# Attention: exponentials ahead of the copies of the transposes, sums of logits behind the next maximum

## The chip, the cores and the metric

The kernel runs on one core of a Trainium2 chip. The core has engines with instruction queues of their own: TensorE (PE in the rows, its weight loads PEld) multiplies matrices, ScalarE (ACT), VectorE (DVE) and GpSimd (POOL) work element by element, and SyncE (SP) issues DMAs here. Each engine takes its instructions in the order of the program and waits on semaphores for those of other engines. Matrix products land in tiles in PSUM; the other tiles of the kernel lie in SBUF. The metric is the device time of one execution in microseconds, the median of three runs.

## What is computed

Three stages follow one another; the change is in the first.

```python
# attention over keys and values averaged in groups of 8: B, H, S, D = 8, 8, 576, 64
k_p = k.reshape(B, H, S // 8, 8, D).mean(axis=3)      # 72 pooled keys a head
v_p = v.reshape(B, H, S // 8, 8, D).mean(axis=3)
scores = np.matmul(q, k_p.transpose(0, 1, 3, 2)) / np.sqrt(D)
attn = np.exp(scores - np.max(scores, axis=-1, keepdims=True))
attn = attn / (np.sum(attn, axis=-1, keepdims=True) + 1e-09)
x = np.matmul(attn, v_p).transpose(0, 2, 1, 3).reshape(B * S, H * D)   # 4608 x 512
# mixture of experts: a skip score decides whether a token is computed, a gate (8 logits) by
# which expert; out = x + gate_w * (relu(x @ w1[e]) @ w2[e])
# rational feed-forward: h = x @ w_in; g = P(h) / Q(h); out = g @ w_out
```

## The kernel before

**Tiles of tokens.** The 4608 tokens are cut into 36 tiles of 128. For each pair of batches there are nine: two blocks of 256 tokens of the first batch (each gives two tiles, the even and the odd tokens), one mixed tile (64 tokens of either batch), and two blocks of the second. A mixed tile needs the keys of two batches, so its score matmuls and its products with v come in twice the number.

**One step of the loop.** The loop runs over `i` from -2 to 35, and its program order is the order on every engine; nothing reorders it. A step works on five tiles at once, in this order:

- `st_B(i + 1)`: TensorE makes the scores of a tile (L392) in the PSUM tile `sc`; VectorE takes the maxima of the eight heads in one reduction (L402). In eight of the steps, one for each batch, TensorE also multiplies the pooled v by the gate's weights (L359) into the same PSUM tile, behind the scores, and VectorE multiplies the result by a mask (L365) behind the maximum. So the product with v gives, beside the 64 columns of a head, its share of the 8 expert logits, of the skip score and of the sum of the exponentials.
- `st_A(i + 2)`: TensorE transposes q (L376) in the PSUM tile with the tag `qT`, ScalarE copies it to SBUF (L378).
- `st_C(i - 1)`: TensorE transposes the exponentials (L421, and L422 for the last 64 of 576) in the PSUM tiles `eT` and `ms`; ScalarE copies both (L424, L425).
- `st_exp(i + 1)`: ScalarE makes the exponentials, eight instructions of 128x72 (L414), one for each head with its own maximum as bias.
- `mark`: VectorE makes two one-hot tables for a tile whose rank is known (L529, L531).
- `st_D(i - 2)`: TensorE multiplies the transposed exponentials by v (L439) in the PSUM tile `pv`.
- `advance`: the router's next stage for a finished group of 8 or 4 tiles. In its third stage TensorE counts tokens by expert (L510) in columns of `ms`; in its fourth VectorE reads them (`val`, L518).
- `finish(i - 2)`, which `st_D` returns: VectorE adds and inverts the sums (L454, L456), scales the logits (L457) and the 512 columns (L460), sums the logits over the heads into `lg` (L466) and into the token's row `xr` (L467), and SyncE stores the rows of a finished pair to `xg` in DRAM (L471, L473). There are two `xr` buffers, one for a pair.
- Behind it: TensorE places the marked tokens (L535), and in certain steps prepares a later batch: it transposes its pooled keys in the PSUM tile `eT` (L332) and the last 64 rows of them in `ms` (L338), and its pooled v in `qT` (L346). ScalarE copies the results (L313, L318, L349).

**What exists once.** The PSUM tiles of this stage are `sc` and `pv` with 2 x 512 numbers in each partition, and `qT`, `eT`, `ms` and the placing table `ix` with 512. Each of them has one buffer. The transposes of keys share theirs with those of the exponentials, the transposes of v with those of q, and the columns of `ms` are shared by three users:

```python
ps = ps1.tile([128, 512], F32, tag="eT", name="kTp")      # prep_k: pooled keys
ps = ps1.tile([128, 4, 128], F32, tag="eT", name="eTp")   # st_C: exponentials
ps = ps1.tile([128, 512], F32, tag="qT", name="vTp")      # prep_v: pooled v
ps = ps1.tile([128, 512], F32, tag="qT", name="qTp")      # st_A: q
ET4, RK0, CN0, KT4 = 0, 264, 345, 354                     # columns of ms
```

Of the kernel before, what the change touches and what calls it, by code (L numbers as in the profile page):

```python
# [26 lines left out]
NT = NTOK // 128  # L27
# [76 lines left out]
def tile_attention_moe_rational_ffn(  # L104
# [92 lines left out]
    with ExitStack() as c1, tc.manual_schedule():  # L197
# [123 lines left out]
        def warm(n):  # L321

            for _ in range(n):
                nc.tensor.transpose(MS[:, 0:128], ident, ident)

        def prep_k(bb):
            kb, kt = kT[bb]
            ps = ps1.tile([128, 512], F32, tag="eT", name="kTp")
            for c in range(4):
                if bb == 0:  # L330
                    warm(6)
                nc.tensor.transpose(ps[:, 128 * c:128 * c + 128], kb[:, c].rearrange("p m d -> p (m d)"), ident)  # L332
            head_block(kt, ps, 0, 512)
# [73 lines left out]
        def st_exp(t):  # L407

            kind, bb, s0, par = TILES[t]
            scv, mx = sc.pop(t)  # L410
            for a in range(2):
                for m in range(4):
                    r, h = (0, 4 * a + m) if kind == "mixed" else (m % 2, 4 * par + 2 * a + m // 2)
                    nc.scalar.activation(out=ex[t][:, r, SP * h:SP * h + SP], in_=scv[:, a, m], func=AF.Exp,  # L414
                                         bias=mx[:, a, m:m + 1], scale=1.0)
# [15 lines left out]
        def st_D(t):  # L431
            ps = ps1.tile([128, 2, 512], F32, tag="sc" if t in (NT - 3, NT - 1) else "pv", name="pvp")
            et = eT.pop(t)
            for p0, n, bb in segs(t):
                for c, h0, nh in PV:
                    np_ = 128 if c < 4 else 64
                    a, hh_ = divmod(h0, 4)
                    m0 = h0 - HEAD0[c]
                    nc.tensor.matmul(ps[p0:p0 + n, a, W * hh_:W * (hh_ + nh)], et[:np_, c, p0:p0 + n],  # L439
                                     vb[bb][:np_, c, m0:m0 + nh, :].rearrange("p m w -> p (m w)"),  # L440
                                     start=h0 in (0, 4), stop=c == 4, skip_group_check=True)
            pv = ps[:, :, 0:4 * W].rearrange("p a (h w) -> p a h w", w=W)
            kind, bb, s0, par = TILES[t]
            if par == 0:
                xr[t] = wk.tile([128, 2, ROW], F32, tag="xr", name="xr")
                if kind == "block":
                    xr[t + 1] = xr[t]
            x_ = xr.pop(t)
            r = wk.tile([128, 2, 4], F32, tag="rs", name="rs")
            l_ = wk.tile([128, H, E + 1], F32, tag="lp", name="lp")  # L450
            rb = r.unsqueeze(3)

            def finish():
                V.tensor_scalar(out=r, in0=pv[:, :, :, W - 1], scalar1=1e-9, scalar2=float(POOL),  # L454
                                op0=ALU.add, op1=ALU.mult)
                V.reciprocal(out=r, in_=r)  # L456
                V.tensor_tensor(out=l_.rearrange("p (a h) e -> p a h e", a=2), in0=pv[:, :, :, D:D + E + 1],  # L457
                                in1=rb.to_broadcast([128, 2, 4, E + 1]), op=ALU.mult)
                if t < NT - 2:
                    V.tensor_tensor(out=x_[:, par, 0:DM].rearrange("p (a h d) -> p a h d", a=2, h=4),  # L460
                                    in0=pv[:, :, :, 0:D], in1=rb.to_broadcast([128, 2, 4, D]), op=ALU.mult)
                else:
                    for h in range(H):
                        nc.scalar.activation(out=x_[:, par, D * h:D * h + D], in_=pv[:, h // 4, h % 4, 0:D], func=AF.Copy,
                                             scale=r[:, h // 4, h % 4:h % 4 + 1])
                V.tensor_reduce(out=lg[:, t, :], in_=l_.rearrange("p h e -> p e h"), axis=AX.X, op=ALU.add)  # L466
                V.tensor_reduce(out=x_[:, par, DM:ROW], in_=l_[:, :, 0:E].rearrange("p h e -> p e h"), axis=AX.X,  # L467
                                op=ALU.add)
                r0 = S * bb + s0
                if kind == "mixed":  # L470
                    nc.sync.dma_start(xg[r0:r0 + 128, :], x_[:, 0, :])  # L471
                elif par:
                    nc.sync.dma_start(xg[r0:r0 + 256, :].rearrange("(p r) f -> p r f", r=2), x_)  # L473

            return finish
# [88 lines left out]
        groups = [(0, 8), (8, 16), (16, 24), (24, 28), (28, 32), (32, 36)]  # L564
        todo = []
        put = []
        prep_k(0)
        warm(6)
        prep_k4(0)
# [8 lines left out]
        for i in range(-2, NT):  # L578
            if i + 5 < NT and i + 5 > 5 and TILES[i + 5][3] == 0:
                load_q(i + 5)  # L580
            for bb in range(B):
                if bb < 2:
                    continue
                if i == max(need[bb] - 11, -2):
                    load_kv(bb, "k")
                if i == need[bb] - 7:
                    load_kv(bb, "v")
                if i == need[bb] - 8:
                    pool_k(bb, nc.gpsimd, nc.gpsimd)()
                if i == need[bb] - 5:  # L590
                    pool_v(bb, (nc.gpsimd, nc.gpsimd))
            if i == 0:
                zero_kt(2, V)
                for c in range(5):
                    rows, n = slice(D * (c % 2), D * (c % 2) + D), min(3, H - HEAD0[c])
                    V.tensor_copy(wg[rows, c, 0:n], wga[rows, HEAD0[c]:HEAD0[c] + n])
            if i == 2:
                V.tensor_copy(tri, cst[:, C_TRI:C_TRI + 128])
                V.tensor_copy(reg, cst[0:1, C_REG:C_REG + NE])
            if i == 3:  # L600
                V.tensor_scalar(out=iob[:, :, 0], in0=iota[:, 0:128], scalar1=-1.0, scalar2=None, op0=ALU.mult)
            if i == 4:
                V.tensor_scalar(out=colb[:, :, 0], in0=iota, scalar1=128.0, scalar2=float(-64 * NCOL), op0=ALU.mult, op1=ALU.add)
            if i == 6:
                nc.sync.dma_start(ab[:, 0:4], a.unsqueeze(0).to_broadcast([128, 4]))
                nc.sync.dma_start(ab[:, 4:6], b.unsqueeze(0).to_broadcast([128, 2]))
            if i == 10:
                nc.gpsimd.tensor_scalar(out=na, in0=ab[:, 0:4], scalar1=-1.0, scalar2=None, op0=ALU.mult)
                nc.scalar.activation(out=bb1, in_=ab[:, 5:6], func=AF.Abs)
            if i == NT - 10:  # L610
                for n in range(NR):
                    load_w(n)
            if i == -1:
                warm(10)
            if 0 <= i + 1 < NT:
                st_B(i + 1, [bb for bb in range(B) if i == need[bb] + (1 if bb else 2)])
            if 0 <= i + 2 < NT:
                st_A(i + 2)
            if 0 <= i - 1 < NT:
                st_C(i - 1)  # L620
            if 0 <= i + 1 < NT:
                st_exp(i + 1)
            if i == 2:
                pool_v(1, (V, V))
            made = [mark(todo.pop(0)) for _ in range(min(len(todo), 1 if i < 28 else 2))]
            ended = st_D(i - 2) if 0 <= i - 2 < NT else None
            for _ in range(1 if i < 32 else 2):
                advance()
            if ended:
                ended()  # L630
            for p_ in put:
                place(*p_)
            if i == 1:
                rest1()
            for bb in range(B):
                if bb and i == need[bb] - (4 if bb > 1 else 2):
                    prep_k(bb)
                if bb and i == need[bb] - (3 if bb > 1 else 2):
                    prep_k4(bb)
                if i == need[bb] - (2 if bb > 1 else 0 if bb else -1):  # L640
                    prep_v(bb)
            put = made
            for g in groups:
                if i - 2 == g[1] - 1:
                    running.append((route(*g), g))
            if NT - 4 <= i < NT:
                split_w(i - NT + 4)
# [4 lines left out]
        for p_ in put:  # L652
            place(*p_)
        ends = [st_D(NT - 2), st_D(NT - 1)]
        ends[0]()
        while len(todo) > 2:
            place(*mark(todo.pop(0)))
        ends[1]()
        for _ in route(*groups[-1]):
            if todo:  # L660
                place(*mark(todo.pop(0)))
# [41 lines left out]
    with ExitStack() as c3, tc.manual_schedule():  # L703
# [271 lines left out]
        ended, begun, uf = small(NU, E), small(NU, E), small(NUT)  # L975
# [107 lines left out]
    with ExitStack() as c4, tc.manual_schedule():  # L1083
# [22 lines left out]
        late = {}  # L1106
# [224 lines left out]
```

## Time and profile before

| | |
|---|---|
| Median of three runs | 1521.79 us (1521.28 to 1528.7) |
| The profiled execution | 1520.28 us, span 1518.5 us |
| Granted TensorE clock, mean over the span | 0.963 |
| TensorE matmuls busy | 1390.6 us (92%) |
| VectorE busy | 1116.5 us (74%) |
| ScalarE busy | 889.2 us (59%) |
| GpSimd busy | 642.4 us (42%) |

The shares are means over all three stages. Scores are made between 13.2 and 199.2 us, so what the change touches is the first eighth of the span; the experts and the feed-forward come behind it and are not touched. A matmul is shown in pipelined form, and the shares are to be read for a stretch, together with what each engine waited for.

### The profile page before, as it was taken

The numbers are of one execution on the slowest core, as the hardware profiler recorded it, in microseconds if no ns is written. First come the engines' busy times: TensorE is split into PE (matmuls) and PEld (weight loads), VectorE is DVE, ScalarE is ACT, GpSimd is POOL, SyncE is SP. The second block draws the span as 40 slices with busy tenths as digits, with TensorE's granted clock in tenths as the row PEclk, the third lists the DMA queues.
The fourth block names the chain that finished last, engine by engine and source line by source line (L and its number), as shares of the span: only waits on it lengthen the run. The fifth ranks groups of instructions, "written<-read, shape, count | busy, mean of one in ns | idle before, by whom it ended". The sixth has DMA issues, their size and how long they took to land.

```text
span 1518.5 us, 21279 instructions
## 1 busy us (share of the span) xinstructions
PE 1390.6 (92%) x6937; PEld 1158.6 (76%) x6937; DVE 1116.5 (74%) x1926; ACT 889.2 (59%) x1805; POOL 642.4 (42%) x575
## 2 busy tenths in 40 slices
PE   7999977879778789997799999999999999999998
PEld 6887856667667677785578888888888888888886
DVE  5478785676667675536998787787878878787885
ACT  4666644344444444335677676776767667676764
POOL 4856226555444443334754233252423325242322
PEclk9999998899979899999999999999999999999999
DMA  9675525556666565341101001010100101010000
GB/s 260 192 223 181 179 76 195 176 184 191 200 209 204 180 209 197 123 129 46 42 1 44 13 28 29 1 56 1 42 14 29 29 1 57 0 43 15 28 1 28
DMA packets 83823, 146.43 MB, mean 96 GB/s; under 512 B 17030, under 2 KB 33866, under 8 KB 83526
## 3 DMA queue, kind: packets, MB, share of 16 engines
q1 hardware_dynamic: 71846, 105.65, 21.7%
q0 software_dynamic: 11680, 37.64, 7.8%
q8 instruction: 86, 1.41, 0.4%
q14 instruction: 211, 1.73, 0.4%
HBM read 117.15 MB, written 27.18 MB: 95 GB/s over the span
## 4 chain that ended last, share of the span: by engine, by line
PE 47%; DVE 5%; ACT 1%; issue 1%; POOL 0%; POOLq 0%; DVEq 0%; ACTq 0%
PE ph L1164 23%; PE py L1222 23%; DVE A L1178 1%; PE px L1147 1%; DVE R L1205 1%; DVE A L1197 1%; DVE R L1201 1%; ACT R L1192 0%; DVE U L1186 0%; ACT R L1193 0%; DVE U L1182 0%; DVE cm L147 0%; POOL out_dram L1228 0%; ACT U L1174 0%; ACT Y L1173 0%
## 5 line engine op out<-in xcount | busy, mean ns | idle before, releaser
L1212 POOL TENSOR_TENSOR GL<-R,GH 128x512 fp32r<-128x512 f32 x143 | 188.0, 1314 | 463.2 <-ACT GH L1211 339.0
L1222 PE MATMUL py<-w0h,GL 128*128 128x512 f32 x576 | 225.2, 391 | 6.6 <-POOL GL L1212 6.6
L1222 PE MATMUL py<-w0h,GH 128*128 128x512 f32 x576 | 226.8, 394 | 0.6 <-issue 0.6
L161 POOL TENSOR_TENSOR w2l<-raw,w2h 128x512 fp32r<-128x512 f32 x90 | 122.3, 1363 | 182.6 <-ACT w2h L160 133.0
L1172 ACT ACTIVATE A<-ph 128x512 f32<-128x512 f32 x140 | 83.0, 593 | 140.7 <-PE ph L1164 140.4
L1178 DVE SCALAR_TENSOR_TENSOR A<-A,bb,Y 128x512 f32<-128x512 f32 x144 | 119.8, 832 | 53.4 <-ACT Y L1173 53.4
L1164 PE MATMUL ph<-xh,w1h 128*128 128x512 f32 x356 | 139.9, 393 | 6.3 <-DVE U L1186 6.3
L1197 DVE SCALAR_TENSOR_TENSOR A<-A,R 128x512 f32<-128x512 f32 x144 | 112.8, 783 | 37.0 <-ACT R L1193 31.0
L1164 PE MATMUL ph<-xl,w1h 128*128 128x512 f32 x356 | 139.4, 392 | 0.0
L1222 PEld LDWEIGHTS py<-w0h,GL 128*128 128x128 f32 x576 | 108.1, 188 | 32.7 <-POOL GL L1212 9.6
L1222 PEld LDWEIGHTS py<-w0h,GH 128*128 128x128 f32 x576 | 108.2, 188 | 22.8 <-issue 0.9
L1211 ACT ACTIVATE GH<-R 128x512 fp32r<-128x512 f32 x144 | 91.9, 638 | 50.8 <-DVE R L1205 50.8
L1205 DVE SCALAR_TENSOR_TENSOR R<-U,ab,R 128x512 f32<-128x512 f32 x144 | 113.1, 785 | 5.1
L1201 DVE SCALAR_TENSOR_TENSOR R<-A,R 128x512 f32<-128x512 f32 x144 | 101.8, 707 | 15.9
L1192 ACT ACTIVATE R<-A,qc 128x512 f32<-128x512 f32 x144 | 104.8, 728 | 14.6 <-DVE A L1178 11.1
L1174 ACT ACTIVATE U<-ph,na 128x512 f32<-128x512 f32 x140 | 109.8, 784 | 0.0
L1186 DVE SCALAR_TENSOR_TENSOR U<-U,ab,ph 128x512 f32<-128x512 f32 x140 | 104.7, 748 | 5.0
L833 PE MATMUL py<-w2h,hh 128*128 128x512 f32 (+2 forms) x240 | 98.9, 412 | 2.4 <-DVE lrow L808 2.4
L845 ACT ACTIVATE hh<-ph 128x256 fp32r<-128x256 f32 (+4 forms) x44 | 19.7, 448 | 136.9 <-PE ph L842 92.1
L833 PE MATMUL py<-w2h,hl 128*128 128x512 f32 (+2 forms) x240 | 96.9, 404 | 2.6 <-DVE hl L846 2.6
L842 PE MATMUL ph<-xh,w1h 128*128 128x256 f32 (+4 forms) x176 | 64.4, 366 | 37.3 <-issue 32.8
L846 DVE SCALAR_TENSOR_TENSOR hl<-ph,hh 128x256 fp32r<-128x256 f32 (+4 forms) x44 | 22.1, 502 | 102.2 <-ACT hh L845 81.6
(328 smaller groups left out, 3812.6 us busy)
## 6 DMA issues: line engine op xcount, KB each, us to landing
raw<-in_moe_w_dram SPq DMA_DIRECT2D x192, 256.0 KB
xg<-xr SPq DMA_DIRECT2D x16, 520.0 KB
q<-in_q_dram SPq DMA_DIRECT2D x16, 512.0 KB
cr<-in_moe_w_in_dram SPq DMA_DIRECT2D x16, 512.0 KB
cr<-in_moe_w_out_dram SPq DMA_DIRECT2D x16, 512.0 KB
k<-in_k_dram SPq DMA_DIRECT2D x7, 1024.0 KB
v<-in_v_dram SPq DMA_DIRECT2D x7, 1024.0 KB
xg<-xr SPq DMA_DIRECT2D x4, 260.0 KB
```

The costliest lines, as they stand in the source:

```text
L161: eng.tensor_tensor(out=dst_lo, in0=src, in1=dst_hi, op=ALU.subtract)
L833: nc.tensor.matmul(PY[j][0:m], l_[:, sl], r_, start=f == 0 and n == 0, stop=f == 7 and n == 2)
L1164: nc.tensor.matmul(ps, l_, r_, start=n == 0, stop=n == 11)
L1174: nc.scalar.activation(out=t["U"], in_=ps, func=AF.Identity, scale=na[:, 3:4], bias=na[:, 2:3])
L1178: nc.vector.scalar_tensor_tensor(out=t["A"], in0=t["A"], scalar=bb1, in1=t["Y"], op0=ALU.mult, op1=ALU.add)
L1186: nc.vector.scalar_tensor_tensor(out=t["U"], in0=t["U"], scalar=ab[:, 1:2], in1=t["h"], op0=ALU.subtract, op1=ALU.mult)
L1192: nc.scalar.activation(out=t["R"], in_=t["A"], func=AF.Ln, bias=qc, scale=1.0)
L1197: nc.vector.scalar_tensor_tensor(out=t["A"], in0=t["A"], scalar=QC, in1=t["R"], op0=ALU.add, op1=ALU.mult)
L1201: nc.vector.scalar_tensor_tensor(out=t["R"], in0=t["A"], scalar=2.0, in1=t["R"], op0=ALU.subtract, op1=ALU.mult)
L1205: nc.vector.scalar_tensor_tensor(out=t["R"], in0=t["U"], scalar=ab[:, 0:1], in1=t["R"], op0=ALU.subtract, op1=ALU.mult)
L1212: (nc.gpsimd if s < tot_ - 1 else nc.vector).tensor_tensor(out=GL, in0=t["R"], in1=GH, op=ALU.subtract)
L1222: nc.tensor.matmul(PY[j], l_[:, sl], r_, start=c == 0 and n == 0, stop=c == NC - 1 and n == 2)
```

## The change

On ScalarE the eight exponentials of a tile (`st_exp`) come ahead of the copy of the transposed q (`st_A`) and of the copies of the transposed exponentials (`st_C`). TensorE's order stays. On VectorE the last part of `finish`, the two sums over the heads, becomes a function `rest`, which runs in the next step behind the next maximum (and behind the mask products L365, where the step has them). The store on SyncE's queue goes with it, and so comes behind the loads of q, k and v that the next step issues. From step 35 on, and for the last two tiles, `rest` runs at once.

```diff
--- before.py
+++ after.py
@@ -463,6 +463,9 @@
                     for h in range(H):
                         nc.scalar.activation(out=x_[:, par, D * h:D * h + D], in_=pv[:, h // 4, h % 4, 0:D], func=AF.Copy,
                                              scale=r[:, h // 4, h % 4:h % 4 + 1])
+                return rest
+
+            def rest():
                 V.tensor_reduce(out=lg[:, t, :], in_=l_.rearrange("p h e -> p e h"), axis=AX.X, op=ALU.add)
                 V.tensor_reduce(out=x_[:, par, DM:ROW], in_=l_[:, :, 0:E].rearrange("p h e -> p e h"), axis=AX.X,
                                 op=ALU.add)
@@ -564,6 +567,7 @@
         groups = [(0, 8), (8, 16), (16, 24), (24, 28), (28, 32), (32, 36)]
         todo = []
         put = []
+        late = []
         prep_k(0)
         warm(6)
         prep_k4(0)
@@ -614,12 +618,14 @@
                 warm(10)
             if 0 <= i + 1 < NT:
                 st_B(i + 1, [bb for bb in range(B) if i == need[bb] + (1 if bb else 2)])
+            if late:
+                late.pop()()
+            if 0 <= i + 1 < NT:
+                st_exp(i + 1)
             if 0 <= i + 2 < NT:
                 st_A(i + 2)
             if 0 <= i - 1 < NT:
                 st_C(i - 1)
-            if 0 <= i + 1 < NT:
-                st_exp(i + 1)
             if i == 2:
                 pool_v(1, (V, V))
             made = [mark(todo.pop(0)) for _ in range(min(len(todo), 1 if i < 28 else 2))]
@@ -627,7 +633,9 @@
             for _ in range(1 if i < 32 else 2):
                 advance()
             if ended:
-                ended()
+                late.append(ended())
+                if i >= NT - 1:
+                    late.pop()()
             for p_ in put:
                 place(*p_)
             if i == 1:
@@ -652,10 +660,10 @@
         for p_ in put:
             place(*p_)
         ends = [st_D(NT - 2), st_D(NT - 1)]
-        ends[0]()
+        ends[0]()()
         while len(todo) > 2:
             place(*mark(todo.pop(0)))
-        ends[1]()
+        ends[1]()()
         for _ in route(*groups[-1]):
             if todo:
                 place(*mark(todo.pop(0)))
```

## Rows read from the trace of the kernel before

**Rows 1.** Busy time by stretches: length, engines' busy time, clock, DMA share, GB/s.

```profile
60.00:80.00 20.00, 18.63 (x134) 16.38 (x133) 11.35 (x39) 14.21 (x56) 14.37 (x15) 1.00 0.55 161
```

**Rows 2.** Maxima and exponentials, 44 to 190 us: who waited for them, us, times.

```profile
  DVE vb L365: 1.7, 1
...
  PE scp L392: 4.9, 10
```

**Rows 3.** Timeline of one ordinary step: start us, length us, engine, line; idle time before.

```profile
60.87 1.25 PE L392 MATMUL scp<-kT,qTs 128*128 128x144 f32 x8
...
61.45 0.27 DVE L466 TENSOR_REDUCE lg<-lp 128x9 f32<-128x72 f32 x1
...
61.64 0.25 DVE L467 TENSOR_REDUCE xr<-lp 128x8 f32<-128x64 f32 x1
...
62.22 0.76 DVE L402 TENSOR_REDUCE mx<-scp 128x8 f32<-128x576 f32 x1 [0.33 <-PE scp L392]
...
62.65 0.60 ACT L378 ACTIVATE qTs<-qTp 128x512 f32<-128x512 f32 x1 [1.35 <-PE qTp L376]
...
62.93 2.02 PE L439 MATMUL pvp<-vb,eTs 128*128 128x148 f32 x12
...
63.14 0.59 ACT L424 ACTIVATE eTs<-eTp 128x512 f32<-128x512 f32 x1
...
63.62 0.26 ACT L425 ACTIVATE eTs<-ms 64x128 f32<-64x128 f32 x1
...
63.78 1.76 ACT L414 ACTIVATE ex<-scp,mx 128x72 f32<-128x72 f32 x8
...
65.58 0.39 PE L392 MATMUL scp<-kT,qTs 128*128 128x144 f32 x1 [0.64 <-ACT ex L414]
```

**Rows 4.** Timeline of TensorE alone, 50 to 88 us.

```profile
52.35 3.67 PE L439 MATMUL pvp<-vb,eTs 128*64 128x148 f32 x24
...
60.16 0.44 PE L346 MATMUL vTp<-ident,vc 128*128 128x128 f32 x2
...
69.60 0.66 PE L332 MATMUL kTp<-ident,kb 128*128 128x128 f32 x4
...
70.31 1.25 PE L392 MATMUL scp<-kT,qTs 128*128 128x144 f32 x8
...
75.78 1.25 PE L392 MATMUL scp<-kT,qTs 128*128 128x144 f32 x8 [0.58 <-ACT ex L414]
...
85.16 0.21 PE L510 MATMUL ms<-oh,tri 128*128 128x72 bf16 x1
...
85.86 1.25 PE L392 MATMUL scp<-kT,qTs 128*128 128x144 f32 x8
```

**Rows 5.** Views of lines L332 and L338: the semaphore waits of TensorE's queue.

```profile
L332 PEldq EVENT_SEMAPHORE  x1: 51/51/51, 68.5 to 68.5; - x1
...
L338 PEldq EVENT_SEMAPHORE  x1: 51/51/51, 74.1 to 74.1; - x1
```

**Rows 6.** Timeline of ScalarE alone, 56 to 92 us.

```profile
67.86 0.59 ACT L424 ACTIVATE eTs<-eTp 128x512 f32<-128x512 f32 x1
...
73.82 0.26 ACT L425 ACTIVATE eTs<-ms 64x128 f32<-64x128 f32 x1
```

**Rows 7.** Timeline of VectorE alone, two stretches.

```profile
72.27 0.76 DVE L402 TENSOR_REDUCE mx<-scp 128x8 f32<-128x576 f32 x1 [0.93 <-PE scp L359]
...
72.95 0.35 DVE L365 TENSOR_TENSOR vb<-scp,cst 128x108 f32<-128x108 f32 x2
...
88.91 0.23 DVE L518 TENSOR_TENSOR val<-ms,oh 128x72 f32<-128x72 f32 x1 [0.93 <-ACT eTs L425]
...
92.47 0.76 DVE L402 TENSOR_REDUCE mx<-scp 128x8 f32<-128x576 f32 x1
```

**Rows 8.** Busy time by stretches, TensorE alone: length, busy time, clock, DMA.

```profile
36.00:38.00 2.00, 0.79 (x5) 1.00 0.08 30
...
38.00:40.00 2.00, 1.63 (x7) 0.61 0.00 0
```

## The prediction

> **What bounds the kernel now.** The change lies in the attention stage, the first 0.2 ms of the span, so I read that stage alone. First the busy time by stretches: between 60 and 80 us TensorE is busy 18.63 of 20 us at its full clock [rows 1]. TensorE nearly sets the pace, and what the change can win is what is left of its waits. Then the view of the maxima and exponentials between 44 and 190 us: TensorE's scores waited for exponentials 10 times, 4.9 us in all [rows 2]. Then one ordinary step in the timeline [rows 3]. Counted from its first score matmul (60.87) the scores end at 1.25, VectorE's maximum runs from 1.35 to 2.11, ScalarE copies the transposed q from 1.78 to 2.38 and the transposed exponentials from 2.27 to 2.86 and 2.75 to 3.01, and runs the exponentials from 2.91 to 4.67; the product with v ends at 4.08, and the next scores start at 4.71. So a ring is closed: scores, transposes of q, three copies, eight exponentials, scores. ScalarE has no gap in it from the first copy on, and the maximum is ready 0.80 before the exponentials start. TensorE stood still 0.64 at the end of this step. Where other work comes after the product, that gap is filled and TensorE itself is the limit.
>
> **The change part by part.** No instruction is added or taken away; two orders change.
>
> *Exponentials first.* They can start about 0.05 after the maximum, at 2.16, and end at 3.92. The copy of q starts 0.10 before that end (as the exponentials now start 0.10 before the end of the copy ahead of them) and runs from 3.82 to 4.42, the copies of the transposed exponentials from 4.31 to 4.90 and 4.79 to 5.05. The next scores need the copy of q and can start at 4.46. A bare step gains 0.25. But all three copies now end about two microseconds later in the step, and what waits for them is the next question. Four things do, because their PSUM tiles exist once:
>
> - The transposes of the pooled keys of a later batch (L332) write the tile that the copy L424 reads. Now that copy ends at 68.45 and TensorE's queue passes the wait of L332 at 68.5, a microsecond before the product ends and the transposes start at 69.60 [rows 4 to 6]: hidden by the product. In the new order the copy ends at 4.90, after the product's 4.08.
> - The transposes of the pooled v (L346) write the tile that the copy of q reads: 4.42 against 4.08.
> - The transposes of the last 64 key rows (L338) and the router's count matmuls (L510) write the tile `ms` that the copy L425 reads. The wait of L338 is passed at 74.1, and L425 ended at 74.08 [rows 5, 6].
> - VectorE's product `val` (L518) reads `ms`. At 88.91 it stood 0.93 for L425, although it reads other columns [rows 7].
>
> All of these stand ahead of the next scores in TensorE's order, or, for `val`, ahead of the normalisation and the next maximum in VectorE's. The Trainium skill, "PSUM — Partial Sum Buffer", section "PSUM bank collisions raise a hardware error", says that two engines may not touch one bank in one quarter of the partitions at once, also at other columns, and that software must order them. The wait of `val` (0.93) agrees; by that rule the sum is the one below, and with an order by columns alone it would be that of the first rival.
>
> Now the sum, over the steps from 44 us on; the counts come from the loop (batches 2 to 7 each bring one step with L332, one with L338, one with L346 and one in which the scores are followed by the products L359).
>
> 1. Steps with nothing after the product, six, and two whose scores are of a mixed tile: 8 x -0.25 = -2.0.
> 2. L332 in three plain steps: it starts at 4.95, and the next scores 0.71 later (69.60 to 70.31), at 5.66. Now such a step takes 4.73 (65.58 to 70.31) [rows 3, 4]: 3 x 0.93 = 2.8.
> 3. L332 in three steps with L359: there the maximum starts at 1.96 instead of 1.35 (72.27 after 70.31) [rows 4, 7], 0.61 later, and VectorE's two products out of the same tile, 0.35 [rows 7], stand before the exponentials, which once waited 1.7 us for them [rows 2] and no longer have copies to cover it. So 5.66 + 0.96 = 6.62 against 5.47 now (70.31 to 75.78): 3 x 1.15 = 3.4.
> 4. L346: it starts at 4.47, and the scores 0.71 later (60.16 to 60.87) [rows 3, 4], at 5.18 against 4.72. Of six steps one also has the count matmuls (term 6): 5 x 0.46 = 2.3.
> 5. L338: three of six are in steps whose product is of a mixed tile, 3.67 long instead of 2.02 [rows 3, 4]; it ends near 5.8 and hides the wait. One is in term 6. Two are in steps with L359: 5.05 + 0.96 + 0.05, some 0.25 for the transposes, 6.3 against 5.47: 2 x 0.85 = 1.7.
> 6. L510, four times inside the loop: 5.10 instead of about 4.08 after a plain product, 6.06 instead of 4.69 (4.08 + 0.61) with L359: 2 x 1.0 + 2 x 1.35 = 4.7. Its own 0.70 (85.16 to 85.86) [rows 4] is there before and after.
> 7. `val`, three times: L425 ends 2.04 later. The step at 85.86 is the dear one: the maximum after it (92.47, 6.61 after the scores) follows VectorE's work without a wait [rows 4, 7]. It becomes later by 2.04, less 0.44 for the reductions below, while its scores come 0.25 earlier: 1.8. For the other two, whose rows don't stand here, I take 0.5 each, nearer to nothing (VectorE idle before the next maximum, as in rows 3) than to 1.8: 2.8.
>
> Together +15.7.
>
> *Sums of logits behind the next maximum.* Two VectorE reductions (from 61.45 to the end of the second at about 61.89) move behind the maximum: 0.44 in front of it. In rows 3 the maximum still waited for the scores after them, so this is worth nothing in an ordinary step and 0.44 only where VectorE is late; it is in term 7. With them the store of each finished pair on SyncE's queue moves behind the next step's loads. By the offsets above it is issued some 1.6 later (now about 1.0 after the next scores start, then about 2.6); the pair's buffer comes back soonest around the four mixed tiles, so at most 4 x 1.6 = 6 us if nothing hid it. I take nothing, since a whole step lies between, and keep 6 for the range.
>
> *The first steps.* Up to 44 us the copy of the next q is put behind the eight exponentials, which bounds the loss at 1.76 + 0.60 = 2.4 for the first step; the stage also waits for loads there (TensorE busy 0.79 of the 2 us from 36 [rows 8]), so I take nothing. After the loop the order is as before, and the rest of the kernel moves by the sum.
>
> The profiled execution took 1520.28 (span 1518.5), so 1536.0; the median of the runs is 1.5 above it: 1521.8 + 15.7 = 1537.5.
>
> **The rivals.** *Only the two big tiles count* (chance 0.10): the order on `ms` is looser than `val` suggests. Terms 1 to 4 remain: +6.5, 1528. Against it stand rows 5 to 7, where two users of `ms` moved on at L425's end.
>
> *The new waits are hidden* (0.10), the other side: one mechanism, the ring of copies gets shorter and the transposes L332, L338 and L346 still come late enough. It decides as soon as the copies end before 4.08; they would have to run 0.8 earlier than in my chain. Then the gain is at most TensorE's 4.9 of waits [rows 2]: 1517 to 1521. Against it: eight exponentials of 1.76 cannot shrink. That the new order does nothing would end here too.
>
> *More than the sum* (0.20): TensorE loses its clock, or VectorE's lateness is handed on. Between 36 and 38 us TensorE was busy 0.79 of 2 us, and from 38 the granted clock was 0.61 of 2.4 GHz, nearer the 1.2 GHz level [rows 8]. The gap behind `val` is the longest new one. A stretch of 4 us at 0.61 costs 1.6; three of them, or half of the bound for the stores together with the first steps' 2.4, give +20 to +21, 1542, and all bounds together 1546 or more.
>
> **How the numbers follow.** My forecast, all four kinds of wait, has 0.60, and its own range is 1532 to 1542. From 1526 the range takes in the first rival and leaves out the second; up to 1547 it holds most of the third. What a measurement of this kernel can tell from no change is about 0.5%, 7.6 us. The first rival and most of the second fall inside, with a little of the forecast's lower end: 0.18. The rest of the second is faster: 0.03. Slower: 0.79.
>
> **What would show it.** In the profile after, exponentials should start 0.05 after each maximum, and L332, L338, L346, L510 should show TensorE waiting for L424, L425 or L378, 0.3 to 1.3 each; `val` should stand about 2 us for L425, three times. Bare steps should take about 4.5. The attention stage should end some 15 us later, and all after it should keep its length. The prediction is wrong if those transposes start right at the end of the product as now, or if the stage after attention takes up the delay.

## The result

The changed kernel takes 1539.72 us (median of 6 runs, 1535.5 to 1542.02) and the kernel before, timed beside it, 1524.38 us (median of 6, 1521.28 to 1528.7): 15.3 us more, or 1.0101 of before. The ratio on record, worked out from the runs and not from the two medians, is 1.0112 with a 95% interval of 1.0083 to 1.0142, which is 12.7 to 21.6 us. Forecast were 15.7 more. The profiled execution of the changed kernel took 1541.26 us with a span of 1539.5, so the two profiled executions lie 21.0 apart, 5.7 more than the medians. The runs of the changed kernel go from 1535.5 us at a mean granted clock of 0.963 to 1542.02 at 0.958; the profiled one had 0.958, and that of the kernel before 0.963. What follows is a reading of these two; where a term fits the profiles and not the medians, it is said.

The line numbers after L463 moved: the sums L466 and L467 are now L469 and L470, the count matmuls L510 are L513, `val` L518 is L521.

**Where the time is.** The first expert matmuls tell whether the delay is made in attention. The view of their line, weight loads, in the changed kernel (duration in ns, then the first and the last start in us):

```profile
L850 PEld LDWEIGHTS ph<-xh,w1h x176: 186/188/338, 258.1 to 682.9; 128*128 128x128 f32 x176
```

and the same line in the kernel before:

```profile
L842 PEld LDWEIGHTS ph<-xh,w1h x176: 186/188/333, 236.9 to 661.4; 128*128 128x128 f32 x176
```

The first comes 21.2 later and the last 21.5: the whole difference of 21.0 stands there before the experts begin, and what lies behind changes it by no more than 0.5. It comes from three places: 7.7 from the opening, 12.2 from the steps of the loop, and 1.3 from between the last scores and the experts. Most of the last is one wait: TensorE stands 3.04 instead of 1.84 for the last block of rows that are gathered from DRAM for the experts (`gx`, L1000 before and L1008 after), which it takes up 21.29 later, where it took up the block ahead 20.1 later. Why these rows came later was not traced, and the change doesn't touch that order.

**The ring of a step.** The timeline of an ordinary step of the changed kernel, one with nothing behind the product, answers to [rows 3]:

```profile
69.95 1.25 PE L392 MATMUL scp<-kT,qTs 128*128 128x144 f32 x8
...
71.31 0.76 DVE L402 TENSOR_REDUCE mx<-scp 128x8 f32<-128x576 f32 x1 [1.06 <-PE scp L392]
...
71.98 0.27 DVE L469 TENSOR_REDUCE lg<-lp 128x9 f32<-128x72 f32 x1
...
72.10 1.80 ACT L414 ACTIVATE ex<-scp,mx 128x72 f32<-128x72 f32 x8 [1.56 <-DVE mx L402]
...
73.74 0.65 ACT L378 ACTIVATE qTs<-qTp 128x512 f32<-128x512 f32 x1
...
74.22 0.66 ACT L424 ACTIVATE eTs<-eTp 128x512 f32<-128x512 f32 x1
...
74.44 0.76 PE L392 MATMUL scp<-kT,qTs 128*128 128x144 f32 x4 [0.41 <-ACT qTs L378]
```

The reader is to see the new chain in its order. The maximum starts at 1.36 of the step, as before; ScalarE stands for it and starts the exponentials 0.03 after its end, at 2.15; they end at 3.95, the copy of q at 4.44, and the next scores start at 4.49 instead of 4.71. They now name the copy of q (L378) as what they waited for, not the exponentials. So the ring is 0.22 shorter, and TensorE still stands 0.41 in it. The copies of the transposed exponentials now start at 4.27, where they ended at 2.86 and 3.01 before.

**What stands behind the product.** Four steps of TensorE in the changed kernel, which answer to [rows 4] (the moment at the left, the idle time before in brackets):

```profile
79.51 0.63 PE L332 MATMUL kTp<-ident,kb 128*128 128x128 f32 x4 [0.98 <-ACT eTs L425]
79.97 1.15 PE L392 MATMUL scp<-kT,qTs 128*128 128x144 f32 x8
...
85.97 0.24 PE L338 MATMUL ms<-ident,kb 64*128 64x64 f32 x1 [1.26 <-ACT eTs L425]
86.15 1.25 PE L392 MATMUL scp<-kT,qTs 128*128 128x144 f32 x8
...
90.72 0.41 PE L346 MATMUL vTp<-ident,vc 128*128 128x128 f32 x2 [0.49 <-ACT qTs L378]
...
91.24 1.74 PE L392 MATMUL scp<-kT,qTs 128*64 128x144 f32 x16
...
96.81 0.19 PE L513 MATMUL ms<-oh,tri 128*128 128x72 bf16 x1 [0.85 <-ACT eTs L425]
...
97.27 1.23 PE L392 MATMUL scp<-kT,qTs 128*128 128x144 f32 x8
```

and ScalarE's copies there:

```profile
78.71 0.66 ACT L424 ACTIVATE eTs<-eTp 128x512 f32<-128x512 f32 x1
...
79.18 0.29 ACT L425 ACTIVATE eTs<-ms 64x128 f32<-64x128 f32 x1
...
85.54 0.29 ACT L425 ACTIVATE eTs<-ms 64x128 f32<-64x128 f32 x1
...
89.93 0.65 ACT L378 ACTIVATE qTs<-qTp 128x512 f32<-128x512 f32 x1
...
96.47 0.29 ACT L425 ACTIVATE eTs<-ms 64x128 f32<-64x128 f32 x1
```

Each transposition or count starts 0.05 to 0.14 after the end of the copy that the forecast gave for it: L332 after the large copy of the transposed exponentials (L424, 79.37), L338 and the counts after the small one (L425, 85.83 and 96.76), L346 after the copy of q (90.58). Each has TensorE idle before it, where [rows 4] has none before L332, L346 and L510. The timeline names L425 for the wait of L332, but the view of that line has TensorE's queue past its wait at 79.4, before L425 ends at 79.47:

```profile
L332 PEldq EVENT_SEMAPHORE  x1: 51/51/51, 79.4 to 79.4; - x1
```

In all six places the queue passes the wait of L332 0.04 after the end of L424 and before that of L425. In the kernel before it was 0.04 behind L424 as well, so only the moment of the copy changed. A step whose product is of a mixed tile is the control within the same trace:

```profile
61.06 3.67 PE L439 MATMUL pvp<-vb,eTs 128*64 128x148 f32 x24
64.66 0.27 PE L338 MATMUL ms<-ident,kb 64*128 64x64 f32 x1
64.86 1.25 PE L392 MATMUL scp<-kT,qTs 128*128 128x144 f32 x8
```

The same L338 starts here without a wait, as the product lasts until 64.73 and the copy L425 ended at 63.74. The three steps of this kind became 0.10, -0.01 and 0.09 longer.

The waits of the stretch from 52 to 215 us in the changed kernel, in total, times and the longest:

```profile
ACT ex L414 <- DVE mx L402: 38.8, 22, 4.1
...
PE kTp L332 <- ACT eTs L425: 6.1, 6, 1.7
...
DVE val L521 <- ACT eTs L425: 5.4, 3, 2.6
...
PE ms L513 <- ACT eTs L425: 4.2, 4, 1.2
...
PE ms L338 <- ACT eTs L425: 2.3, 2, 1.3
...
PE vTp L346 <- ACT qTs L378: 1.9, 5, 0.5
...
PE scp L392 <- ACT qTs L378: 1.6, 5, 0.4
```

The rows of L332 go to L424, as said above. The counts are those of the forecast: six for L332, four for the count matmuls, two for L338 outside the mixed products, three for `val`. Of the five for L346 one lies in the step ahead of tile 6 (51.88); in the fifth place of the forecast (194.62) the view names no wait, though L346 starts 0.15 after the end of the copy of q (194.47) there too. TensorE waits 6.1 + 4.2 + 2.3 + 1.9 = 14.5 us for copies that it never waited for in these steps before. The largest row, ScalarE's 38.8 for the maxima, is no loss by itself: ScalarE used to stand for the transposes of q in the same place, and the bare step has this wait (1.56) and is shorter.

**The steps one by one.** The starts of the scores of tiles 6 to 35 in the two traces, in us:

```
before  tiles  6 to 15: 44.71 50.19 56.15 60.87 65.58 70.31 75.78 80.50 85.86 90.58
before  tiles 16 to 25: 96.06 102.37 107.09 111.81 116.52 123.90 129.04 134.40 139.12 144.60
before  tiles 26 to 35: 150.80 155.52 160.24 164.96 170.66 175.45 180.81 185.53 191.01 198.09
after   tiles  6 to 15: 52.42 58.80 64.86 69.95 74.44 79.97 86.15 91.24 97.27 101.73
after   tiles 16 to 25: 108.86 115.16 120.25 124.74 130.27 136.45 142.64 147.62 155.52 161.80
after   tiles 26 to 35: 168.10 173.20 177.68 183.21 190.04 195.13 200.29 204.70 211.33 218.00
```

From tile 6 to tile 35 the delay grows from 7.71 to 19.91, by 12.2. Sorted by what the step holds (forecast and measured are sums over the steps of the kind, changed less before; they are taken from starts to the nanosecond and can differ by 0.01 from those above):

| Steps | Forecast | Measured |
|---|---|---|
| bare, or scores of a mixed tile (8) | -2.0 | seven -0.21 to -0.38, sum -1.8; the eighth lies under `val`, put at -0.25 |
| L332 (3) | +2.8 | 0.81 each, +2.4 |
| L332 with L359 (3) | +3.4 | 0.91, 0.81 and about 0.86, +2.6 |
| L346 (5) | +2.3 | 0.37, 0.37, 0.37, 0.38, 0.31, +1.8 |
| L338 with L359 (2) | +1.7 | +0.70 and -1.20, -0.5 |
| count matmuls (4) | +4.7 | 0.67, 1.05, 1.12, 1.15, +4.0 |
| `val` (3) | +2.8 | +0.8, +3.4, 0.0, +4.2 |
| product of a mixed tile (3), last step (1) | 0 | +0.2, -0.4 |
| sum | +15.7 | +12.2 |

The one step that has L332 with L359 and follows a `val` became 1.65 longer; 0.86, the mean of the other two of its kind, is put down to L332, and the rest to `val`. With this split the rows add up to the 12.2; it is a way of booking, and not a measurement of each kind by itself.

**The opening.** Another 7.7 of the profiled difference arise before 53 us. The first steps of TensorE in the changed kernel:

```profile
17.05 1.25 PE L392 MATMUL scp<-kT,qTs 128*128 128x144 f32 x8 [3.05 <-ACT qTs L378]
...
22.57 2.29 PE L392 MATMUL scp<-kT,qTs 128*128 128x144 f32 x8 [3.83 <-ACT qTs L378]
```

and in the kernel before:

```profile
15.49 1.25 PE L392 MATMUL scp<-kT,qTs 128*128 128x144 f32 x8 [0.69 <-ACT qTs L378]
...
17.92 1.25 PE L392 MATMUL scp<-kT,qTs 128*128 128x144 f32 x8 [0.75 <-ACT qTs L378]
```

The scores of tiles 1 and 2 wait 3.05 and 3.83 for a copy of q that now stands behind eight exponentials, and come 1.56 and 4.65 later. As the very first scores start 0.80 earlier than before (12.42, not 13.22), the first step is 2.36 longer and the second 3.09. In the second the maximum, too, is late: VectorE's copies of the gate's weights stand before it (L600 in the rows below), and it starts at 19.45, 1.15 after its scores end. Tile 3 is 4.33 late, and then VectorE's pooling of v for batch 1 falls into GpSimd's pooling of k for batch 2. VectorE and GpSimd in the changed kernel:

```profile
16.74 2.80 DVE L600 COPY wg<-wga 64x27 f32<-64x27 f32 x5 [0.76 <-DMA wga<-in_moe_w_skip_dram]
...
31.52 4.56 POOL L266 TENSOR_TENSOR k<-k 128x1024 f32<-128x1024 f32 x2 [7.07 <-DMA k<-in_k_dram]
...
32.57 4.05 DVE L294 TENSOR_TENSOR v<-v 128x1024 f32<-128x1024 f32 x2
...
44.27 0.74 DVE L402 TENSOR_REDUCE mx<-scp 128x8 f32<-128x576 f32 x1
```

VectorE in the kernel before:

```profile
29.67 1.95 DVE L294 TENSOR_TENSOR v<-v 128x1024 f32<-128x1024 f32 x2 [1.32 <-DMA v<-in_v_dram]
...
35.73 0.74 DVE L402 TENSOR_REDUCE mx<-scp 128x8 f32<-128x576 f32 x1
```

The two large adds take 4.05 instead of 1.95 and the next (36.66) 1.37 instead of 0.42, while GpSimd adds arrays of the same shape; before, VectorE was through with v when GpSimd began (33.37). The Trainium skill, "SBUF — State Buffer", section "Who interferes with whom", says that a VectorE instruction with two inputs in SBUF and a GpSimd instruction that reads SBUF exclude each other; the longer adds agree with it. The meeting is not VectorE's lateness alone: GpSimd itself began 1.85 earlier than before, when its load of k had landed. Had it begun at 33.37, VectorE's adds from 32.57 on, at their old length of 1.95, would still have run into it by 1.15 (an estimate from these rows). The maximum of tile 4 comes 8.5 later, and some of that is made up by tile 6. TensorE's clock has a part as well. In the kernel before the granted clock was low around 26 us (0.60 over 24 to 28) and 40 us (0.61 and 0.54 over 38 to 42); in the changed one around 24 us (0.57 over 22 to 26), 30 us (0.63 over 28 to 32) and 44 us (0.68 and 0.50 over 42 to 46; 0.50 is the lower of the two levels, 1.2 GHz). The last of these came after TensorE had stood 2.60 for VectorE, and the product at 42.48 took 3.71 where the same product took 2.02 before. How the 7.7 divide between late copies, VectorE and GpSimd, loads and the clock is not shown.

### The profile page after: what moved, and what is told of

Same layout as the page of the kernel before. It is cut to its first block, busy times and chain, and to the rows that moved or that the text cites. A ratio compares the mean times of both kernels' runs of the same rounds, so it can differ in the third digit from the quotient of the medians.

```text
span 1539.5 us, 21264 instructions
## 1 busy us (share of the span) xinstructions
PE 1395.2 (91%) x6937; PEld 1162.8 (76%) x6937; DVE 1111.5 (72%) x1926; ACT 887.5 (58%) x1805; POOL 645.6 (42%) x575
## 3 DMA queue, kind: packets, MB, share of 16 engines
q1 hardware_dynamic: 71846, 105.65, 21.6%
## 4 chain that ended last, share of the span: by engine, by line
PE 47%; DVE 5%; ACT 1%; issue 1%; POOL 0%; POOLq 0%; DVEq 0%; ACTq 0%
PE ph L1172 23%; PE py L1230 23%; DVE A L1186 1%; PE px L1155 1%; DVE A L1205 1%; DVE R L1213 1%; DVE R L1209 1%; ACT R L1200 0%; DVE U L1194 0%; ACT R L1201 0%; DVE U L1190 0%; DVE cm L147 0%; POOL out_dram L1236 0%; ACT U L1182 0%; ACT Y L1181 0%
## 5 line engine op out<-in xcount | busy, mean ns | idle before, releaser
L414 ACT ACTIVATE ex<-scp,mx 128x72 f32<-128x72 f32 x288 | 64.7, 336 | 77.7 <-DVE mx L402 58.6
```

## The experiments

No variant of the kernel was measured: none of those that were set out has a time or a trace, and what the text calls shown rests on the two traces above. Three of the edits follow, with what each theory expects of them on record; beside them the moved sums alone, and the kernel before without the preparation, were set out. They say what would settle the points that stay open: what the sums are worth, what each wait costs by itself, and what the opening costs.

The first undoes the move of the sums and keeps the new place of the exponentials:

```diff
-                return rest
-
-            def rest():
                 V.tensor_reduce(out=lg[:, t, :], in_=l_.rearrange("p h e -> p e h"), axis=AX.X, op=ALU.add)
...
-            if late:
-                late.pop()()
...
```

> Exponentials ahead of the copies, but the two sums over the heads stay ahead of the next maximum. My theory (copies that end late hold up whatever shares their PSUM tiles, and the opening loses too): about as slow as the whole change, 1.007 to 1.016 of before, and the same steps lose the same amounts (about 0.8 where L332 follows the product, 0.4 where L346 does, 1.0 where L510 does); up to 0.44 more in steps where VectorE is late. Rival (the moved sums, with the later store, are what costs): within 0.3% of before.

The second leaves the preparation of batches 2 to 7 out of the kernel before and of the changed one alike (the keys and the v of batches 0 and 1 are used again), so that nothing is left behind the product but the count matmuls:

```diff
         def prep_k(bb):
+            if bb > 1:
+                return
...
         def prep_k4(bb):
+            if bb > 1:
+                kT[bb] = kT[bb - 2]
+                return
...
```

> The changed kernel with the same work left out as in the run before this one. My theory: the steps that lost behind L332, L346 and L338 now gain 0.2 to 0.3 each against the run before, as bare steps do; what is left from step 5 on is the wait of the count matmuls and of the product val, so the last scores come about 12 - 7 = 5 us later than in the run before, counted from step 5, where the whole change showed 12.2. Rival (the ring through VectorE's maximum is slower by itself): still about 12.

The third puts one copy back to its old place and leaves the other two late:

```diff
             if 0 <= i + 2 < NT:
                 st_A(i + 2)
+            if 0 <= i + 1 < NT:
+                st_exp(i + 1)
             if 0 <= i - 1 < NT:
                 st_C(i - 1)
-            if 0 <= i + 1 < NT:
-                st_exp(i + 1)
```

> The kernel before with one thing changed: ScalarE copies the transposed q first, as before, then makes the exponentials, and only then copies the transposed exponentials; the sums stay where they were. So one of the copies is back at its old time and the other two stay late, by half a microsecond less than in the changed kernel (their ends at 4.53 and 4.68 of a step). My theory (what waits for a late copy is what loses): no wait of L346 for the copy of q, and its steps as long as before within 0.1; L332 still waits, some 0.5, and its steps lose 0.5 to 0.8; L510 waits some 0.65; val waits 1.6 to 2 more than before; bare steps gain 0.3 to 0.55, since the next scores need only the end of the exponentials at 4.04. Over steps 5 to 35 some +6 in place of +12, the opening about as before: 1.001 to 1.006 of before. Rival one (the moved sums and the later store are what costs): within 0.2% of before and no waits of L332 or L510. Rival two (the ring through VectorE's maximum is slower by itself, whatever the copies do): all steps lose alike, bare ones too, 1.007 or more.

## Why the prediction was right, point by point

**The ring.** Forecast were exponentials 0.05 after the maximum and scores at 4.46; the trace has 0.03 and 4.49, and bare steps of 4.49 instead of 4.71. The gain was 0.22 to 0.31 in the five bare steps outside `val`, where 0.25 was forecast. So the rival of the second experiment, that the ring through the maximum is slower by itself, is out.

**The four waits.** All four stand in the trace in the forecast places, and the waiting instruction starts right behind the copy that the prediction gave for it, L332 behind L424 too. This is shown by the traces, and the mixed products, which hide the waits in the same trace, are the check on it. The first rival, that `ms` is ordered more loosely, is out: the count matmuls waited for L425 four times and `val` three times. The second `val` waited only 0.28 and not the forecast two, because VectorE came to it late.

**The sizes.** Terms 2 to 4 were too large by 1.7 together (8.5 forecast, 6.8 measured). The step that failed is the "0.71" from L332, and from L346, to the next scores: in the rows of before that time also held the last of a wait for the exponentials. In the changed kernel the scores follow L332 after 0.46 (79.51 to 79.97) and L346 after 0.52 (90.72 to 91.24); both start 0.1 later in the step than forecast, which takes back a part. Term 6 was too large by 0.7: the first of the four comes after the scores of a mixed tile and lost only 0.67, and the two with L359 lost 1.12 and 1.15 where 1.35 was put.

Term 5 and term 7 met something that the sum did not hold: VectorE instructions that run long while GpSimd works, at other places than before. That GpSimd holds them up is argued from the overlap in time, and no experiment shows it. The kernel before has this row, which runs into the step of the second L338 with L359 (116.52 to 123.90):

```profile
114.97 4.57 DVE L494 TENSOR_TENSOR val<-val,cst 128x64 f32<-128x64 f32 x1
...
117.11 3.69 POOL L266 TENSOR_TENSOR k<-k 128x1024 f32<-128x1024 f32 x2
```

and the changed kernel has in its place:

```profile
128.20 0.23 DVE L497 TENSOR_TENSOR val<-val,cst 128x64 f32<-128x64 f32 x1
```

where GpSimd does nothing (126.6 to 137.1), so that a step that should have lost 0.85 became 1.20 shorter. The other way round, around the second `val`, VectorE and GpSimd in the changed kernel show:

```profile
145.19 3.85 POOL L266 TENSOR_TENSOR k<-k 128x1024 f32<-128x1024 f32 x2
...
145.53 2.08 DVE L532 TENSOR_SCALAR ma<-iob,low,cst 128x128 bf16<-128x128 bf16 x1
...
148.19 0.23 DVE L521 TENSOR_TENSOR val<-ms,oh 128x72 f32<-128x72 f32 x1 [0.28 <-ACT eTs L425]
...
149.12 1.28 POOL L274 TENSOR_TENSOR kb<-k 128x512 f32<-128x512 f32 x1
...
149.19 1.24 DVE L526 TENSOR_SCALAR top<-rnd 128x8 f32<-128x8 f32 x1
...
151.52 0.75 DVE L402 TENSOR_REDUCE mx<-scp 128x8 f32<-128x576 f32 x1
```

where the table `ma` takes 2.08 and the last rank step 1.24, 0.34 and 0.16 in the same step of the kernel before (other VectorE instructions there run at their usual length beside the same adds); the maximum starts 3.90 after its scores instead of 1.29, and the step is 3.2 longer than before, 3.4 with the 0.25 that a bare step gains. A part of it is TensorE's clock, below. At the first and the third `val` the wait for L425 itself is 2.58 each, close to the forecast two:

```profile
102.31 0.23 DVE L521 TENSOR_TENSOR val<-ms,oh 128x72 f32<-128x72 f32 x1 [2.58 <-ACT eTs L425]
...
104.38 0.75 DVE L402 TENSOR_REDUCE mx<-scp 128x8 f32<-128x576 f32 x1
```

The first cost 0.8 and not 1.8, because VectorE had 0.89 of work from `val` to the normalisation (102.31 to 103.20) where it had 1.93 before (88.91 to 90.84).

**The opening.** This is the term that was wrong. It was taken as nothing, on the ground that the stage waits for loads, with a bound of 2.4 for the first step. In the profiled execution it cost 7.7. The bound held for the first step (2.36), but the second step paid again and more (3.09), and then VectorE's pooling met GpSimd's. How much of the 7.7 the median run pays is open: the medians differ by 15.3, and if the steps from tile 6 on cost 12.2 in every run as in the profiled pair, some 3 are left for opening and rest. Whether loads arrive at other times from run to run was not measured; in the two traces GpSimd's load of k came 1.85 apart.

**The moved sums.** In the bare step the two sums run in front of idle time (from 71.98 on; VectorE's next instruction starts at 74.07), and no row has VectorE waiting for a store. Where VectorE is late the move should help as forecast: in the steps of the first and the second `val` the maximum follows the normalisation without a wait (104.38, 151.52), and the two sums, 0.44 long before, would have stood between. That they are worth little is argued from this, not shown, as no kernel with that part alone was timed.

**The third rival.** Between 48 and 220 us TensorE's clock fell once, to 0.91 over 140 to 160 us, the stretch of the second `val`, where the kernel before has 1.00 (length, TensorE busy, clock, DMA share, GB/s):

```profile
140.00:160.00 20.00, 17.09 (x120) 0.91 0.50 159
```

The product there:

```profile
151.75 3.69 PE L439 MATMUL pvp<-vb,eTs 128*128 128x148 f32 x12 [1.90 <-DVE xr L460]
```

TensorE had stood 1.90 before it; the granted clock was 0.50 over 152 to 154 us, the lower level, and the product took 3.69 instead of 2.02. The next scores (155.52) follow its end, while the copy of q had ended at 154.59; behind that copy they would have started at about 154.6, so the clock cost some 0.9 of the 3.4 (an estimate from these rows). The rest goes with VectorE's lateness, which the rival named too. So the third rival has a part in the second `val` and in the opening, and none in the other steps.

The total came out within 0.4 of the forecast, which is luck: in the profiled pair the steps gave 3.5 less than forecast, the opening and the stretch behind the loop gave 9.0 that were not forecast, and the interval of the measured difference is nine microseconds wide. The mechanism in the loop is right; the closeness of the total is not evidence for each term.

## What to carry to other kernels

A chain through several engines can be shortened and the kernel still become slower, if the instruction that is moved back frees a buffer that exists once. Before an instruction is put ahead of a copy, list all who write or read the copied PSUM tile, other columns of it too, and compare the copy's new end with the moment at which each of them is due; here that moment was the end of the product, 4.08 of a step, and copies that ended at 4.4 to 5.0 (later in steps with L359) cost 0.3 to 1.15 a step. A wait that is hidden in the trace of before can be read from the queue's semaphore events: [rows 5] showed both by less than 0.1 us behind the copies, about a microsecond before they were needed. The same events tell which copy a wait was for, where the timeline names only the one that ended last.

## What the runs showed that was not expected

ScalarE's copies show longer behind the exponentials than ahead of them: the copy of q 0.65 instead of 0.60, those of the transposed exponentials 0.66 and 0.29 instead of 0.59 and 0.26. Nothing is lost by it: they overlap more, and start 0.48 and 0.47 after one another (73.74, 74.22, 74.69) where it was 0.49 and 0.48 before (62.65, 63.14, 63.62). Why they overlap more is open. How long VectorE's instructions take went with what GpSimd did at that moment: the same instruction took 4.57 in one trace and 0.23 in the other, another one 2.08 and 0.34, so that single steps differ by up to three microseconds, in either direction. The edit sets this only through the moments at which the two engines meet.
